# RWKV-7 and SwiGLU in one kernel: transposes as pairs of 64-row tiles, narrower Gram products, SwiGLU over two slices, a new order

## The chip, the cores and the metric

One core of a Trainium2 chip runs the whole program. The metric is the device time of one execution in microseconds (us), the median of several runs. In the profile PE is TensorE (its matmuls), PEld its weight loads, DVE is VectorE, ACT ScalarE, POOL GpSimd and SP SyncE, which here only issues DMAs.

## The reference

The first half is a recurrence over 768 tokens for 4 batches of 8 heads with head size 40. For each head there is a 40x40 state:

```python
for t in range(S):
    y[:, :, t] = np.einsum('bhd,bhde->bhe', rt, state)
    Sa = np.einsum('bhde,bhe->bhd', state, at)
    state_decay = state * wt[:, :, None, :] - np.einsum('bhd,bhe->bhde', Sa, bt)
    state = state_decay + np.einsum('bhd,bhe->bhde', vt, kt)
```

The second half takes `y` as 3072 tokens of 320 features, scales them by their root mean square and a gain, and computes `silu(x @ w_gate) * (x @ w_val) @ w_out` with an inner width of 1536. All arrays of the recurrence are float32; the three weight matrices and the gain come in as 64-bit floats and are narrowed to float32 in the kernel.

## The kernel before

**Chunks.** The 768 tokens are cut into 24 chunks of 32 (`C = 32`, `NCH = 24`), and all 32 sequences (4 x 8) are worked on at once. Inside a chunk the recurrence becomes products of small matrices. A step of a chunk is one call of `pe(...)`, `tt(...)`, `copy(...)` and so on; a `pe` step is a list of matmuls that is issued as a whole.

`front(c)` loads w, a, k, b and v of chunk c with the tokens on partitions, turns them round on TensorE (`turned`), and builds the products of keys within the chunk ("Gram" products, `gramk`) in levels of 1, 2, 4, 8 and 16 tokens; DVE scales keys and masks between levels. `inverse(c)` solves a 32x32 triangular system for each sequence on DVE, in 62 steps that depend on one another; the first four chunks (`EARLY`) do a half-sized version and finish on TensorE. `main(c)` carries the state over, forms `y`, and turns `y` twice (`turn4`, `turn3`) so that the features of 128 tokens lie on partitions in `xg`. `feed(g)` takes two chunks (256 columns) through the SwiGLU: 12 slices of 128 inner features in six pairs. For each slice there are two 64-row products (`h64`), four full ones (`h`), a Silu on ACT, a product on DVE and two products into the output (`out`). The weights of a slice come from DRAM (`sW`), 480 KB each, for every group again. `narrow` turns 64-bit weights into these slices at the start, in 24 parts.

**The transposes.** A transpose (`flip`) is a matmul whose stationary operand is the tile to be turned and whose moving operand is an identity. The profile shows it as one instruction at line 489, while every other float32 matmul (line 486) shows as two. `turned` makes eight flips for a tile of 128 partitions and 8 times 104 or 128 columns:

```python
def turned(t, at=lambda n: n, ins=P, outs=TOP):
    ps = plan.room().rearrange("p u f -> p (u f)").rearrange("p (n t) -> p n t", n=N)
    pe("turn", [flip(ps[0:outs, at(n), 0:ins], t[0:ins, n, 0:outs], ident[0:ins, 0:ins]) for n in range(N)])
    return ps
```

In each chunk there are such steps for w and a (`wan`), for k and b (`kbn`), for the scaled keys (`K`, 104 rows), for v and the solved part (`VU`) and for the state (`ST`, 104 rows), and one for r (`rn`) in every second chunk; `turn4` has four flips and `turn3` three.

**What the array is told.** Matmuls come in several tilings of the 128x128 array, which the profile shows as rows*columns of the stationary operand: 128*128 (`h`, `out`, all flips and the fillers), 64*128 (`h64`), 64-row by 64-column tiles (Gram, score, update, y0), 32x32 tiles (`lower`), 128-row by 64-column tiles (`level`) and 64 by 32 (`state`).

**The order.** Nothing is scheduled by the compiler. Every step is first recorded (`Plan.add`); then `Plan.issue` issues all of them in the order of a written-out text `ORDER`, in which each word is the number of a step counted from the first that is not yet issued. Each engine executes its own steps in that order. A "-" in the text issues a filler (`plan.warm`): a matmul of the identity with itself, which is used where TensorE would stand idle. `PAIRS` assigns three pairs of PSUM banks to the steps that ask for a `room`. A fourth pair (`po`) gathers the output of the SwiGLU.

Of the kernel before, what the change touches and what calls it, by code (L numbers as in the profile page):

```python
# [8 lines left out]
I32 = mybir.dt.int32  # L9
# [8 lines left out]
P = 128  # L18
C = 32
LEVELS = (1, 2, 4, 8, 16)  # L20
CG = 2
WB = 5
LEAD = 2
# [10 lines left out]
85 83 84 76 58 78 86 74 73 59 60 75 5 89 61 88 77 4 43 6 201 7 87 334 90 44 8 214 213 53 62 9 - - - - - - - - 93 18 10  # L34
567 335 557 11 12 13 79 14 15 94 566 80 210 16 95 558 108 17 200 - - - 97 96 19 20 100 21 2 22 101 23 98 25 568 202 24
26 107 112 57 - - - - - 102 106 111 124 27 209 122 392 103 109 52 119 113 104 54 578 569 577 155 199 125 110 105 204
120 - - - - - - 114 203 118 117 121 559 211 598 589 562 46 131 129 132 45 560 212 597 563 588 561 123 115 136 586 384
133 134 - - - - - 126 130 116 47 564 3 145 216 394 383 135 336 128 137 48 144 143 141 91 587 219 142 51 570 127 1005
565 146 138 337 55 573 579 281 393 220 582 608 571 390 234 239 607 572 583 580 380 574 251 222 38 221 609 575 581 42 -
- - - - - - - 223 82 226 339 64 379 227 338 39 81 139 224 263 149 576 238 153 56 249 247 590 206 584 228 382 237 591  # L40
593 272 40 233 232 381 154 0 593 32 139 390 204 228 591 388 234 249 247 - - 324 235 35 31 27 244 229 146 147 259 281
245 258 149 34 325 594 36 33 270 155 243 62 605 584 598 230 - 239 40 214 599 601 242 628 64 49 91 627 602 30 626 1135
600 28 48 257 603 29 241 68 150 255 65 0 1347 194 0 194 84 173 0 - - - 182 540 200 0 184 1 186 542 540 0 506 0 457 469
849 199 455 242 111 97 110 112 96 51 61 439 460 458 122 50 243 0 0 255 242 0 709 104 470 242 120 246 259 708 57 247
458 456 0 257 718 256 470 242 0 716 265 487 486 0 268 0 0 265 101 473 0 262 277 0 273 0 236 0 260 0 269 0 242 461 - -
- - - - - 237 0 240 0 278 242 252 0 242 252 0 90 0 0 98 99 246 0 0 230 440 0 230 94 93 457 440 231 - - - - - - - - -
240 441 244 0 44 0 468 440 255 0 450 468 269 469 0 257 214 439 238 213 203 0 257 203 93 449 92 0 0 234 - - - - - - - -
245 437 0 250 262 0 464 246 247 436 260 245 446 258 259 469 244 - - 255 471 465 468 470 466 0 269 215 255 478 466 93
94 264 95 96 266 97 0 97 470 1 2 98 99 0 0 96 467 97 469 98 468 251 265 99 470 100 471 101 441 102 103 258 104 105 260
106 - - - - - - - - - - - 0 106 107 471 108 0 108 502 503 472 0 108 109 110 111 0 0 0 0 0 - - 13 0 16 562 572 146 571  # L50
561 147 14 142 143 374 15 13 355 - - - 25 386 358 0 358 386 388 16 25 387 389 390 70 79 17 391 28 191 147 355 356 80
148 149 359 0 68 28 2 29 149 0 149 34 150 29 151 187 24 25 31 152 33 153 188 391 393 32 154 35 390 392 358 0 0 152 40
187 153 27 154 155 156 33 157 158 159 160 161 34 162 36 163 164 37 165 41 391 38 42 392 39 394 561 166 395 393 552 0
42 559 549 548 395 209 0 549 560 42 165 210 43 44 211 427 428 395 - - - 565 166 45 167 557 168 0 565 566 168 739 0 522
693 534 526 124 - - 0 526 124 139 0 535 681 682 579 0 535 545 547 140 536 138 141 0 547 545 555 543 578 0 558 520 567
- - - - - - 518 378 0 696 378 380 381 695 518 120 685 526 - - - - - - 522 686 379 527 382 136 530 383 554 529 121 - -
141 540 523 565 539 537 142 538 524 - - - - 145 525 148 534 149 152 154 551 535 147 555 - - 157 146 550 536 150 155
# [3 lines left out]
478 595 568 - - 35 830 594 567 820 38 36 - 476 37 571 366 570 0 605 356 433 434 435 436 120 437 0 317 318 319 320 441  # L61
321 322 323 355 456 324 458 459 442 4 357 325 457 326 327 443 328 0 443 328 329 330 331 357 0 35 0 330 2 37 450 359 3
36 358 331 332 357 333 356 0 462 330 461 464 448 331 332 468 364 447 463 31 467 476 458 333 365 334 335 0 425 439 441
302 426 436 0 6 439 2 0 435 332 2 436 443 444 0 448 332 442 334 443 333 340 449 0 32 297 329 342 330 - 3 338 33 341
334 0 332 331 0 332 293 441 0 438 0 436 293 333 336 295 337 309 438 338 1 375 342 310 365 374 515 27 292 0 362 26 28
44 339 29 34 292 27 32 338 0 646 29 34 336 32 0 439 64 315 647 646 339 440 441 63 340 0 287 413 312 313 623 12 414 314
415 315 416 608 624 32 417 480 418 625 419 420 421 316 626 638 33 0 312 417 625 418 - - - - 476 313 601 602 600 610
812 419 420 421 822 258 422 423 0 313 810 423 625 637 2 0 819 2 0 254 473 420 421 645 310 422 0 - - - - - 310 422 3
313 33 0 28 626 307 419 639 627 420 637 308 0 637 20 635 420 647 21 421 23 422 613 648 819 38 22 809 423 39 659 24 611
3 612 36 818 424 651 808 621 425 25 660 426 - 616 249 427 0 427 3 25 58 57 428 28 47 0 428 429 28 430 3 431 0 26 25  # L70
614 484 31 27 617 627 0 458 216 400 590 600 401 0 12 582 32 401 583 25 0 397 579 21 - - - - - - - - - 588 29 28 30 591
22 453 428 398 605 23 0 591 23 429 602 24 609 0 24 397 588 602 1 604 398 429 430 2 399 427 0 584 - - - - - - - - - - -
- - - 4 397 0 25 397 4 0 393 394 21 23 27 28 395 598 24 424 607 0 21 38 35 395 37 396 24 2 424 47 397 398 399 400 25
# [4 lines left out]
663 729 634 977 562 563 717 713 986 978 665 564 565 566 975 567 568 714 569 985 570 571 967 722 572 723 - 0 400 403  # L78
726 402 572 401 573 0 726 738 736 573 739 574 664 575 737 576 577 3 723 578 751 579 760 580 747 581 582 633 583 584 0
584 585 3 634 586 636 587 635 734 588 633 0 746 588 - - - - - 403 757 589 722 590 3 404 591 592 593 594 595 596 408  # L80
# [163 lines left out]
class Plan:  # L244
# [17 lines left out]
    def foot(self, ap):  # L262
# [9 lines left out]
        if key not in self.masks:  # L272
# [4 lines left out]
            self.masks[key] = m  # L277
        return p, p + dims[0][1], self.masks[key]

    def add(self, engine, kind, issue, outs, ins):  # L280
        me = len(self.pieces)
        k = self.count.get(self.stage, 0)
        self.count[self.stage] = k + 1
# [764 lines left out]
```

## Time and profile before

| | |
|---|---|
| three runs | 1061.87, 1062.71 and 1066.75 us, median 1062.71 |
| profiled execution, first to last instruction | 1060.6 us; its own time with what lies around the span is not listed, and the median of the three runs is 2.1 us over the span |
| PE busy | 1009.5 us (95%), 23406 matmuls |
| PEld busy | 829.3 us (78%) |
| DVE busy | 842.3 us (79%), 2861 instructions |
| ACT, POOL busy | 468.1 us (44%), 309.5 us (29%) |
| DMA | 143.35 MB, mean 135 GB/s |

Busy is the time in which at least one instruction of the engine, or of the group, is running. Matmuls overlap each other (one takes 200 to 450 ns from its start to its modelled end, but the next starts long before that), so what a step costs TensorE is read from the timeline: the start of the next step less its own start. The start column of the timeline is used for that below.

### The profile page before, as it was taken

The numbers are of one execution on the slowest core, as the hardware profiler recorded it, in microseconds if no ns is written. First come the engines' busy times: TensorE is split into PE (matmuls) and PEld (weight loads), VectorE is DVE, ScalarE is ACT, GpSimd is POOL, SyncE is SP. The second block draws the span as 40 slices with busy tenths as digits, with TensorE's granted clock in tenths as the row PEclk, the third lists the DMA queues.
The fourth block names the chain that finished last, engine by engine and source line by source line (L and its number), as shares of the span: only waits on it lengthen the run. The fifth ranks groups of instructions, "written<-read, shape, count | busy, mean of one in ns | idle before, by whom it ended". The sixth has DMA issues, their size and how long they took to land.

```text
span 1060.6 us, 53494 instructions
## 1 busy us (share of the span) xinstructions
PE 1009.5 (95%) x23406; PEld 829.3 (78%) x23406; DVE 842.3 (79%) x2861; ACT 468.1 (44%) x1043; POOL 309.5 (29%) x554
## 2 busy tenths in 40 slices
PE   7868999999999999999999999999999999999997
PEld 6767777777888778787778778787777888787875
DVE  8978878776868988898898798989889899787411
ACT  6856666643543534434443444434344443431211
POOL 8824413120532241241233241340331331110000
PEclk9777998999999999999999999999999999999999
DMA  9965458766565483655565555574555555443252
GB/s 168 216 155 133 77 127 207 211 123 178 127 140 126 106 173 96 150 134 125 123 155 129 135 132 114 122 160 119 137 126 126 138 137 138 100 132 102 80 162 68
DMA packets 172457, 143.35 MB, mean 135 GB/s; under 512 B 125504, under 2 KB 143872, under 8 KB 172224
## 3 DMA queue, kind: packets, MB, share of 16 engines
q1 hardware_dynamic: 153856, 116.96, 42.9%
q0 software_dynamic: 16192, 22.64, 12.1%
q8 instruction: 184, 3.01, 1.2%
q10 hardware_dynamic: 2176, 0.33, 0.3%
q14 instruction: 49, 0.40, 0.1%
HBM read 123.86 MB, written 15.99 MB: 132 GB/s over the span
## 4 chain that ended last, share of the span: by engine, by line
PE 72%; DVE 8%; DMA 4%; ACT 3%; issue 3%; POOL 2%; SPq 1%; DVEq 0%; ACTq 0%; POOLq 0%
PE ps L486 50%; PE po L486 13%; PE ps L489 8%; DMA wf<-sW 2%; DVE LT L444 1%; DVE y L444 1%; DVE tmp L444 1%; POOL kbn L483 1%; DVE Yi L444 1%; DVE K L444 1%; SPq L483 1%; DMA sY<-Yi 1%; ACT VU L467 1%; PE po L1015 0%; DVE Ab L444 0%
## 5 line engine op out<-in xcount | busy, mean ns | idle before, releaser
L486 PE MATMUL ps<-xg,wf 128*128 128x256 f32 (+1 forms) x1728 | 353.5, 390 | 4.0 <-DVE xg L444 2.0
L486 PEld LDWEIGHTS ps<-xg,wf 128*128 128x128 f32 (+1 forms) x1728 | 261.4, 188 | 57.2 <-issue 15.0
L486 PE MATMUL po<-wf,hT 128*128 128x320 f32 x576 | 183.1, 449 | 0.1
L464 ACT ACTIVATE sg<-ps 128x256 f32<-128x256 f32 x144 | 53.6, 382 | 228.2 <-PE ps L486 224.9
L444 DVE TENSOR_TENSOR tmp<-Yi,M 128x60 f32<-128x60 f32 (+24 forms) x620 | 130.7, 211 | 19.1 <-DMA M<-sB 5.9
L444 DVE TENSOR_TENSOR Yi<-Yi,tmp 128x60 f32<-128x60 f32 (+24 forms) x620 | 129.7, 209 | 12.7
L483 POOL DMA_DIRECT2D VU<-in_v_dram x92 | 53.2, 584 | 274.1 <-PE ps L486 141.8
L486 PEld LDWEIGHTS po<-wf,hT 128*128 128x128 f32 x576 | 102.5, 191 | 35.7 <-issue 4.1
L444 DVE TENSOR_TENSOR hT<-ps,sg 128x256 f32<-128x256 f32 x144 | 59.7, 420 | 67.2 <-ACT sg L464 66.4
L444 DVE TENSOR_TENSOR K<-K,T 128x512 f32<-128x512 f32 (+1 forms) x192 | 93.4, 496 | 8.3 <-PE ps L486 5.8
L486 PEld LDWEIGHTS ps<-Ab,K 40*64 40x64 f32 x4608 | 77.2, 138 | 28.1 <-issue 10.5
L467 ACT COPY K<-K 128x256 f32<-128x256 f32 (+1 forms) x168 | 71.7, 443 | 58.4 <-PE ps L486 39.2
L486 PE MATMUL ps<-Ab,K 40*64 40x56 f32 x4608 | 87.2, 224 | 9.7 <-issue 3.8
L444 DVE TENSOR_TENSOR As<-ps,msi 128x256 f32<-128x256 f32 (+1 forms) x186 | 78.9, 476 | 14.4 <-PE ps L486 13.8
L467 ACT COPY KN<-ps 128x640 f32<-128x640 f32 x96 | 66.1, 690 | 53.5 <-PE ps L489 23.3
L483 POOL DMA_DIRECT2D kbn<-in_b_dram x92 | 53.3, 583 | 96.7 <-PE ps L486 94.3
L486 PEld LDWEIGHTS ps<-As,KN 128*40 128x40 f32 x3072 | 66.5, 124 | 15.7 <-issue 10.4
L483 POOL DMA_DIRECT2D kbn<-in_k_dram x92 | 53.6, 585 | 82.7 <-PE ps L486 82.6
L486 PE MATMUL ps<-As,KN 128*40 128x32 f32 x3072 | 73.2, 205 | 3.1 <-issue 2.5
L483 POOL DMA_DIRECT2D wn<-in_w_dram x92 | 51.6, 567 | 62.7 <-DVE tmp L444 24.1
L444 DVE TENSOR_TENSOR y<-y,ps 128x256 f32<-128x256 f32 x119 | 50.0, 420 | 16.2 <-PE ps L486 13.7
L444 DVE COPY_PREDICATED LT<-near,ps 128x384 f32<-128x384 uint32 (+2 forms) x72 | 52.2, 725 | 2.6 <-PE ps L486 2.0
(133 smaller groups left out, 1546.0 us busy)
## 6 DMA issues: line engine op xcount, KB each, us to landing
wf<-sW SPq DMA_DIRECT2D x144, 480.0 KB, 3.9
M<-sB SPq DMA_DIRECT2D x80, 128.0 KB, 4.1
rn<-in_r_dram SPq DMA_DIRECT2D x24, 160.0 KB, 5.4
sW<-ex SPq DMA_DIRECT2D x16, 240.0 KB, 3.4
out_dram<-o SPq DMA_DIRECT2D x48, 80.0 KB, 4.2
kbn<-in_k_dram POOLq DMA_DIRECT2D x92, 40.0 KB, 3.9
kbn<-in_b_dram POOLq DMA_DIRECT2D x92, 40.0 KB, 4.1
wan<-in_a_dram POOLq DMA_DIRECT2D x46, 80.0 KB, 4.9
```

Of the source, the lines that this page charges most:

```text
L444: plan.add("DVE", kind, lambda at: fn(at(o), *m(at)), [o], aps(*args))
L464: plan.add("ACT", "act", lambda at: nc.scalar.activation(at(o), at(a), f, **kw), [o] + aps(acc), [a])
L467: plan.add("ACT", "copy", lambda at: nc.scalar.copy(at(o), at(a)), [o], [a])
L483: plan.add(by, "dma", lambda at: queue.dma_start(out=o, in_=i), [o], [i])
L486: return o, lhsT, rhs, lambda at: nc.tensor.matmul(at(o), lhsT, rhs, start=start, stop=stop, skip_group_check=True)
L489: return o, i, ident, lambda at: nc.tensor.transpose(at(o), i, ident)
```

## The change

- `turned` takes its tile as two halves of 64 partitions (or of 40 where the rest is padding) and makes 16 flips instead of 8. The two halves of a pair use the upper and the lower 64 rows of the array and write two different PSUM banks. A flip now moves 64 columns of the identity (40 for `K` and `ST`) where it moved 128 (104). `turn4` goes from 4 to 8 flips of 40 columns, `turn3` from 3 to 6 of 64. The layouts of `rE`, `r2` and `vut` follow, and the copy of `a` into `A` and `Ab` is made in four pieces instead of two.
- The Gram products of the levels 4, 8 and 16 load 60, 56 and 48 key columns instead of 64.
- In `feed`, both slices of a pair go through one Silu and one product of 512 columns instead of two of 256.
- The ring of weight slices has 6 tiles instead of 5, in group 0 only two of them serve the products, and the narrowing uses fixed tiles; `x` and `ex` have fewer buffers, `tmp` is half as wide.
- `ORDER` and `PAIRS` are new throughout. The text has 175 fillers where it had 151.

```diff
-WB = 5
-LEAD = 2
+WB = 6
...
-    def turned(t, at=lambda n: n, ins=P, outs=TOP):
-        ps = plan.room().rearrange("p u f -> p (u f)").rearrange("p (n t) -> p n t", n=N)
-        pe("turn", [flip(ps[0:outs, at(n), 0:ins], t[0:ins, n, 0:outs], ident[0:ins, 0:ins]) for n in range(N)])
+    def turned(t, at, outs=TOP, by=half, w=64):
+        ps = plan.room().rearrange("p u (n t) -> p u n t", n=N)
+        pe("turn", [flip(ps[0:outs, u, at(n), 0:w], t[by(u), n, 0:outs], ident[by(u), by(u)]) for n in range(N) for u in range(2)])
...
-            pe("gramk", [mm(gr[half(i), o, n, 0:16 + D], K[part(o), 2 * n + i].rearrange("p x s -> p (x s)"),
+            pe("gramk", [mm(gr[i * 64:i * 64 + 64 - l, o, n, 0:16 + D], K[part(o), 2 * n + i].rearrange("p x s -> p (x s)")[:, 0:64 - l],
                             A[part(o), 2 * n + i, 16:]) for n, i, o in each])
...
-             turned(K.rearrange("p (n i) x s -> p n (i x s)", i=2), ins=TOP, outs=P).rearrange("p n (o e) -> p n o e", o=2)[:, :, :, 0:D])
+             turned(K.rearrange("p (n i) x s -> p n (i x s)", i=2), lambda n: n, P, part, D).rearrange("p o n e -> p n o e")[:, :, :, 0:D])
...
-        pe("turn4", [flip(xn[:, m], y.rearrange("p (m c) t -> p m (c t)", m=4)[:, m], ident) for m in range(4)])
+        pe("turn4", [flip(xv[:, o, m], yt[part(o), m], ident[part(o), part(o)]) for m in range(4) for o in range(2)])
...
-        pe("turn3", [flip(ps[:, kt, :], x[:, kt * P:(kt + 1) * P], ident) for kt in range(KT)])
+        pe("turn3", [flip(ps[:, u, kt], x[half(u), kt * P:(kt + 1) * P], ident[half(u), half(u)]) for kt in range(KT) for u in range(2)])
...
             for e in range(2):
-                pe("h", [mm(h[e][:, q], wk[e][2 * q + kt], x[:, kt, :], False, kt == 1)
-                                           for q in range(2) for kt in range(2)])
-                act(sgs[:, e], h[e][:, 0], AF.Silu)
-                tt(hTs[:, e], h[e][:, 1], sgs[:, e], MUL)
-                pe("out", [mm(po[:, q, 0:DM], hTs[:, e, q * P:(q + 1) * P], wfs[e][:, 2 * P:2 * P + DM], f + e == 0, f + e == FT - 1)
-                                            for q in range(CG)])
+                pe("h", [mm(h[e][:, q], wk[e][2 * q + kt], x[:, kt, :], False, kt == 1) for q in range(2) for kt in range(2)])
+            act(sg, hh[:, 0], AF.Silu)
+            tt(hT, hh[:, 1], sg, MUL)
+            for e in range(2):
+                pe("out", [mm(po[:, q, 0:DM], hT[:, e * GT + q * P:e * GT + (q + 1) * P], wfs[e][:, 2 * P:2 * P + DM], f + e == 0, f + e == FT - 1)
+                           for q in range(CG)])
...
+    for f in range(FT):
+        narrow_slice(f)
     for c in range(-2, NCH):
```

More of the change, by code (lines that the diff above doesn't have):

```diff
@@ L278, in foot, with add @@
         return p, p + dims[0][1], self.masks[key]
-    def add(self, engine, kind, issue, outs, ins):
+    def add(self, engine, kind, issue, outs, ins, after=()):
         me = len(self.pieces)
@@ L489, in flip, with pe @@
         return o, i, ident, lambda at: nc.tensor.transpose(at(o), i, ident)
-    def pe(kind, steps, more=[]):
+    def pe(kind, steps, more=[], after=()):
         def issue(at):
@@ L494, in issue @@
                 s[3](at)
-        plan.add("PE", kind, issue, [s[0] for s in steps] + more, [x for s in steps for x in s[1:3]])
+        return plan.add("PE", kind, issue, [s[0] for s in steps] + more, [x for s in steps for x in s[1:3]], after)
     ident = const.tile([P, P], FP32, name="ident")
@@ L532 @@
     eye = const.tile([P, C // 4, C], FP32, name="eye")
-    row, column, bits, same = (vut_.tiles[0][:, k, 0:C].bitcast(I32) for k in range(4))
+    row, column, bits, same = (vut_.tiles[0][:, 0, k, 0:C].bitcast(I32) for k in range(4))
     same = same.bitcast(FP32)
@@ L594 @@
     Yi_ = Turns(2, [P, C // 4, C], "Yi")
[L595 to L596 removed]
+    tmp_ = Turns(2, [P, 80], "tmp")
+    rE_ = Turns(1, [P, 2, N, 2 * C], "rE")
     r2_ = Turns(1, [P, N, 2 * C], "r2")
@@ L623 @@
     seq = lambda i, q: slice((i * 2 + q) * N, (i * 2 + q + 1) * N)
+    top = lambda i, x: slice(i * 64 + x * C, i * 64 + x * C + HC)
     own = lambda i, n: rows(i, n // 4)
@@ L900, in main @@
             pe("y0", [mm(y0[part(o), i, n], Sd[part(i), (2 * n + o) * D:(2 * n + o + 1) * D],
-                                 R["rE"][part(o), n, i, tk] if i == o else R["r2"][part(i), n, tk]) for n, i, o in each])
+                                 R["rE"][part(o), i, n, tk] if i == o else R["r2"][part(i), n, tk]) for n, i, o in each])
         level(yl[:, 1], 3)
@@ L970, in feed, with wf_next, narrow @@
             dma(out[row:row + CG * C, :].rearrange("(q s) d -> s q d", q=CG), o[at:at + C])
-    def narrow(f, h, dst, srcs):
-        plan.stage = "narrow", 2 * f + h
-        n = dst.shape[1]
-        rw = wf_.next().bitcast(I32).rearrange("p (f w) -> p f w", w=2)[:, 0:n]
-        for to, src, load in srcs:
-            dma(to(rw).rearrange("p (k f) w -> p k f w", k=2) if load == "raw2" else to(rw),
-                src.bitcast(I32).rearrange("(k p) (f w) -> p k f w", k=2, w=2) if load == "raw2"
-                else src.bitcast(I32).rearrange("p (f w) -> p f w", w=2))
+    def wf_next(g, f):
+        return wf_.tiles[f % 2 if g == 0 else (g * FT + f) % WB]
+    words = lambda w: w.bitcast(I32).rearrange("p (f w) -> p f w", w=2)
+    def narrow(f, part, srcs):
+        k = 2 * f + part
+        plan.stage = "narrow", k
+        rw = wf_.tiles[k if k < 2 else 2 + (k - 2) % 4].bitcast(I32).rearrange("p (f w) -> p f w", w=2)
+        for to, src in srcs:
+            dma(to(rw), src)
         lo, hi, top = rw[:, :, 0], rw[:, :, 1], rw.bitcast(I16)[:, :, 3]
-        ex = ex_.next()[:, 0:n]
+        ex = ex_.next()[:, 0:WH]
         exf, low = ex.bitcast(FP32), lo.bitcast(FP32)
@@ L990, in narrow @@
         stt(exf, low, 2.0 ** 20, exf, ADD, MUL)
-        dma(dst, exf)
-    last, cut = slice(2 * P, DM), WF // 2 - 2 * P
+        dma(sW[f][:, part * WH:(part + 1) * WH], exf)
     def narrow_slice(f):
-        f0, f1 = f * P, (f + 1) * P
-        narrow(f, 0, sW[f][:, 0:2 * P + cut], [
-            (lambda t: t[:, 0:2 * P], moe_w_gate[0:2 * P, f0:f1], "raw2"),
-            (lambda t: t[:, 2 * P:], moe_w_out[f0:f1, 0:cut], "rawo")])
-        narrow(f, 1, sW[f][:, 2 * P + cut:], [
-            (lambda t: t[:, 0:DM - cut], moe_w_out[f0:f1, cut:], "rawp"),
-            (lambda t: t[:, DM - cut:DM - cut + 2 * P], moe_w_val[0:2 * P, f0:f1], "raw2"),
-            (lambda t: t[half(0), DM - cut + 2 * P:], moe_w_gate[last, f0:f1], "raw64"),
-            (lambda t: t[half(1), DM - cut + 2 * P:], moe_w_val[last, f0:f1], "raw64")])
+        gate, value, o = words(moe_w_gate)[:, f * P:(f + 1) * P], words(moe_w_val)[:, f * P:(f + 1) * P], words(moe_w_out[f * P:(f + 1) * P])
+        two = lambda t: t.rearrange("p (k f) w -> p k f w", k=2)
+        pair = lambda w: w[0:2 * P].rearrange("(k p) f w -> p k f w", k=2)
+        cut, last = WH - 2 * P, slice(2 * P, DM)
+        narrow(f, 0, [(lambda t: two(t[:, 0:2 * P]), pair(gate)), (lambda t: t[:, 2 * P:], o[:, 0:cut])])
+        narrow(f, 1, [(lambda t: t[:, 0:DM - cut], o[:, cut:]),
+                      (lambda t: two(t[:, DM - cut:DM - cut + 2 * P]), pair(value)),
+                      (lambda t: t[half(0), DM - cut + 2 * P:], gate[last]),
+                      (lambda t: t[half(1), DM - cut + 2 * P:], value[last])])
+    for f in range(FT):
+        narrow_slice(f)
     for c in range(-2, NCH):
```

182 lines of the change are left out of this document (96 added, 86 removed), and 320 rows, old and new, of the table ORDER.

## The prediction

> **What bounds the kernel now.** I read the page first: busy time, the slices, the chain that ended last.
>
> ```profile
> span 1060.6 us, 53494 instructions
> ...
> PE 1009.5 (95%) x23406; PEld 829.3 (78%) x23406; DVE 842.3 (79%) x2861; ACT 468.1 (44%) x1043; POOL 309.5 (29%) x554
> ...
> PE   7868999999999999999999999999999999999997
> ...
> PEclk9777998999999999999999999999999999999999
> ...
> PE 72%; DVE 8%; DMA 4%; ACT 3%; issue 3%; POOL 2%; SPq 1%; DVEq 0%; ACTq 0%; POOLq 0%
> ```
>
> TensorE is busy in nearly every slice after the first five, and 72% of the chain is its own work. Next the windows, cut where the stages change. The first product of the SwiGLU (`h64`) is at 130 us by the timeline.
>
> ```profile
> 130.27 1.14 PE L486 MATMUL ps<-xg,wf 64*128 64x256 f32 x8
> ```
>
> ```profile
> core 0: us, PE busy (x) PEld busy (x) DVE busy (x) ACT busy (x) POOL busy (x), PEclk, DMA share, GB/s
> 0.00:130.00 130.00, 105.32 (x2827) 94.63 (x2827) 109.43 (x325) 87.42 (x184) 75.99 (x155) 0.86 0.72 152
> 130.00:313.00 183.00, 177.08 (x4128) 143.53 (x4126) 138.02 (x474) 95.57 (x212) 50.15 (x86) 0.98 0.62 156
> 313.00:874.00 561.00, 548.28 (x13206) 448.14 (x13197) 487.45 (x1712) 235.03 (x532) 169.67 (x290) 1.00 0.57 132
> 874.00:1014.00 140.00, 137.72 (x3071) 112.18 (x3072) 102.45 (x339) 44.34 (x104) 13.71 (x24) 1.00 0.43 113
> 1014.00:1061.00 47.00, 41.13 (x192) 30.84 (x192) 4.91 (x12) 5.72 (x14) 0.00 (x0) 0.99 0.36 109
> ```
>
> Three stretches matter. Up to 130 us no engine is full and fillers pad TensorE: work taken off it there is worth nothing by itself. From 313 to 874 us, seven groups of two chunks, it is busy 97.7% of the time, DVE 86.9%. The last 47 us are SwiGLU alone. So the time from 130 us on follows TensorE's work, with DVE close behind: 80.1 us a group, of which DVE is busy 69.6 us.
>
> **What a step costs TensorE.** Busy time counts overlapping instructions once and mean durations count them several times, so I took start-to-start times from the timeline (first column).
>
> ```profile
> 602.29 1.99 PE L486 MATMUL ps<-xg,wf 128*128 128x256 f32 x8
> 604.21 0.79 PE L486 MATMUL ps<-Xs,LT 32*32 32x40 f32 x64
> 604.93 0.66 PE L489 MATMUL ps<-ident,y 128*128 128x128 f32 x4
> 605.43 1.24 PE L486 MATMUL po<-wf,hT 128*128 128x320 f32 x4
> 606.51 1.89 PE L486 MATMUL ps<-xg,wf 128*128 128x256 f32 x8
> 608.33 0.83 PE L486 MATMUL ps<-VU,KN 64*40 64x40 f32 x64
> 608.96 1.14 PE L486 MATMUL ps<-Ab,K 40*64 40x56 f32 x64
> 610.03 0.55 PE L489 MATMUL ps<-ident,x 128*128 128x128 f32 x3
> 610.44 1.08 PE L489 MATMUL ps<-ident,VU 128*104 128x128 f32 x8
> ```
>
> ```profile
> 430.96 1.89 PE L486 MATMUL ps<-xg,wf 128*128 128x256 f32 x8
> 432.69 1.24 PE L486 MATMUL po<-wf,hT 128*128 128x320 f32 x4
> ```
>
> ```profile
> 515.15 1.04 PE L489 MATMUL ps<-ident,kbn 128*104 128x128 f32 x8
> 516.12 0.79 PE L486 MATMUL ps<-Xs,LT 32*32 32x40 f32 x64
> ```
>
> ```profile
> 573.59 0.88 PE L489 MATMUL ps<-ident,ST 104*104 104x104 f32 x8
> 574.31 0.88 PE L489 MATMUL ps<-ident,K 104*128 104x104 f32 x8
> 575.12 1.15 PE L486 MATMUL ps<-Ab,K 40*64 40x56 f32 x64
> ```
>
> An `h` step takes 1.73 us between steps of its own tiling (430.96 to 432.69), 1.82 where another tiling follows (606.51 to 608.33), and 1.92 where another also precedes (602.29 to 604.21). So leaving a tiling costs 0.09 us, and entering one about 0.10 for a full float32 load, less for small loads (0.06 for `y`, below). The Trainium skill, page "TensorEngine Tiling (Array Packing)", section "Tiling Modes", says that changing the mode drains TensorE. The trace agrees at about 0.09 us a change; the page gives no size.
>
> Eight flips of `kbn` take 0.97 us and are followed by another tiling: 0.88 without that, 0.11 a flip of 128 columns, 0.85 ns a column. `ST` takes 0.72 and `K` 0.81 - 0.09 = 0.72 for eight flips of 104 columns: 0.09 a flip. `y` takes 0.50 for four after another tiling, 0.44 plus 0.06. So flips go by the columns that move, and the load is hidden: `K` loads 128 columns within 0.09 us. How long a flip's load is comes from its rows, beside those of two-instruction matmuls:
>
> ```profile
> L489 PEld LDWEIGHTS ps<-ident,y 128*128 128x128 f32 x96 | 10.8, 141 | 3.7 <-ACT K L467 1.1 <-DVE y L444 0.8 <-DVE hT L444 0.4
> L489 PEld LDWEIGHTS ps<-ident,rn 128*104 128x104 f32 x96 | 10.4, 130 | 1.3 <-ACT KN L467 0.4
> L486 PEld LDWEIGHTS ps<-xg,wf 128*128 128x128 f32 x1152 | 211.0, 190 | 39.4 <-issue 9.9 <-DVE hT L444 0.6
> L486 PEld LDWEIGHTS ps<-Ab,K 40*64 40x64 f32 x4608 | 77.2, 138 | 28.1 <-issue 10.5 <-ACT K L467 3.9 <-DVE tmp L444 2.8
> ```
>
> 24 more columns cost a flip's load 11 ns, 0.46 ns a column: 48 ns for 104 columns, 59 for 128. In the other matmuls 64 more columns cost 52 ns, 0.81 a column.
>
> **Do two halves run beside each other?** No flip does so yet. The nearest row is `h64`, the same 64*128 tiling:
>
> ```profile
> L486 PE MATMUL ps<-xg,wf 128*128 128x256 f32 x1152 | 275.5, 386 | 0.3 <-DVE hT L444 0.3
> ...
> L486 PE MATMUL ps<-xg,wf 64*128 64x256 f32 x576 | 80.4, 400 | 3.6 <-DVE xg L444 2.0 <-ACT VU L467 0.9 <-issue 0.5
> ```
>
> A full product of 256 columns takes 239 ns of busy time, a half one 140: two halves 279, not 478. They run together. So I price a pair of flips at the longer of its moving columns (64: 54 ns; 40: 34) and one load (48 or 59): 56 ns for `wan`, `kbn`, `VU`, `rn`, 59 for `K`, `y`, `x`, 49 for `ST`.
>
> **The sum, part by part, from 130 us on.** Counts of steps are those that stand behind the first `h64` in the two order texts, read against the steps in the order in which the code records them.
>
> Transposes. `wan`, `kbn`, `VU`, `rn`: 0.87 to 0.45, 70 steps, 29.4 us. `K`: 0.71 to 0.47, 20 steps, 4.8. `ST`: 0.71 to 0.39, 21 steps, 6.7. `y`: 0.44 to 0.24, 22 steps, 4.4. `x`: 0.33 to 0.18, 22 steps, 3.3. Together 49 us of the 129 us that line 489 is busy in this stretch:
>
> ```profile
> 130.00:1061.00 931.00, 129.46 (x1046) 109.87 (x1044) 1.00 0.55 133
> ```
>
> Bounds: with moving columns alone (pairs of 54 and 34) 30.8 + 8.8 + 9.2 + 6.7 + 3.6 = 59 us; with loads as long as the `K` row allows (89 ns for 128 columns, 72 for 104) 20.7 + 0 + 2.9 + 1.8 + 1.3 = 27. I take 49, since load and move are each read from a row.
>
> Gram. 64 products take 1.07 - 0.09 = 0.98 us, 61 ns for four that run together, near the load of 64 columns at 0.81 (52). With 60, 56 and 48 columns the load shrinks by 3, 6.5 and 13 ns, of which the last is stopped at some 10 by the 56 moving columns (48 ns): 16 fours x 19.5 ns = 0.31 us a chunk, 19 chunks left: 6 us. Between 0 and 7.
>
> Changes of tiling. All flips leave the tiling of `h` and `out`. The old order changes it 471 times from the first `h64` on, the new one 515 times: the new text puts flips next to `h64` or to one another. 44 changes at 0.09 to leave and some 0.05 to enter: 6 us lost. Were all 155 flip steps to stand alone, up to 310 changes would cost 43 us; the count excludes that.
>
> Fillers from there on are 40 before and 30 after: 2 us gained. Steps that moved across the mark: 1 us.
>
> SwiGLU of two slices. It takes no TensorE work. DVE's product:
>
> ```profile
> L444 DVE TENSOR_TENSOR hT<-ps,sg 128x256 f32<-128x256 f32 x144 | 59.7, 420 | 67.2 <-ACT sg L464 66.4
> ...
> L444 DVE TENSOR_TENSOR As<-ps,msi 128x512 f32<-128x512 f32 x42 | 28.4, 683 | 9.6 <-PE ps L486 9.6
> ```
>
> 144 x 0.420 = 60.5 becomes 72 x 0.683 (another 512-column product from PSUM) = 49.2: 11 us less, 0.9 a group. `out` now waits for a longer Silu and product, about 0.5 us more; the next `h` and the chunk's steps queued ahead of `out` cover it, and at the very end, without them, it costs that 0.5 once. The two extra copies of `a` (48 in all) go to ACT, 44% busy: nothing. One `x` buffer instead of two: the next use is a chunk, 40 us, later: nothing. The weight ring and its loads on SP: TensorE hardly waits for `wf` (row below), so nothing to gain. The start: before the first `h64` stand nearly as many steps as now (DVE 318 after 326, ACT 196 after 180, TensorE without fillers 68 after 67), so I leave it at 130 us.
>
> TensorE's work from 130 us on is then less by 49 + 6 + 2 + 1 - 6 = 52 us. **What is late next is DVE.**
>
> ```profile
> DVE y L444 <- PE ps L486: 8.9, 14, 1.9
> DVE hT L444 <- ACT sg L464: 8.7, 12, 1.3
> ```
>
> ```profile
> PE ps L486 <- DMA wf<-sW: 0.2, 1, 0.2
> ```
>
> The first two rows are of the seven middle groups, the third of the whole span. In the groups most of DVE's longest waits end on TensorE directly or through Silu, so they shrink with it, but not below nothing: of 80.1 us a group 69.6 are busy, 68.7 after. A group that is 4.4 us shorter (52 us over eleven groups and the end) leaves 75.7, with DVE at 91%. Two engines so full wait for each other more; I add 0.6 us a group, 6 in all, bounds 0 and 15. 1060.6 - 52 + 6 = 1014.6; with the 2.1 us between span and median: **1017 us**.
>
> **Rivals.** (a) DVE takes over: its waits stay at 10.5 us a group and only its own 0.9 goes. Eleven groups give 10 us: 1053. For it: 87% busy, and DVE's chain of 62 steps a chunk has its order. Against: its waits end on TensorE. It decides if DVE is over 93% in the middle.
>
> (b) Loads bound the pairs, at the 0.81 ns a column of the other matmuls: 84 ns a pair for 104 columns, 104 for 128. Then the first four kinds gain 70 x 0.20, `ST` 21 x 0.04, `y` and `x` 1 together, and `K` loses 20 x 0.12: 13 us instead of 49. TensorE gains 16 in all and DVE stays slack: 1047. Against: `K` loads 128 columns every 90 ns today. The Trainium skill, page "TensorE: Matmul & The Clock Gate", section "LDWEIGHTS (loading the stationary operand)", has a load take its columns divided by 1.2 in ns, 87 and 107 here, nearly this case; the `K` row contradicts it at 128 columns.
>
> (c) Slower: the halves of a flip pair do not overlap. Then 16 flips cost two of today's halves each time: 0.90 for `wan` and its like (loss 70 x 0.03), 0.94 for `K` (20 x 0.23), 0.78 for `ST` (21 x 0.07), `y` and `x` 0.02 each: 9 us lost, plus 6 for changes, less 9 for Gram, fillers and moved steps, and the order, made for shorter flips, adds waits of some 5: 1074. It decides where a pair takes over 108 ns. Against: `h64`. The change would then not do what its name says.
>
> (d) The new order meets later transfers or longer SwiGLU chains than it allows for: a wait of PE for `hT` or `wf` of 0.5 us in each of 72 pairs gives back 36 us: 1053. Against: no such wait now.
>
> **How the numbers follow.** Forecast 0.68, (a) 0.14, (b) 0.05, (c) 0.08, (d) 0.05. 0.5% is 5.3 us, about what a measurement of this kernel can tell. The forecast's own range is 1003 (no new waits, and 8 of the 10 us up to the upper bound of the flips) to 1032 (waits at 15, flips 6 less). To hold 8 in 10 it reaches into (a) and (d): 1003 to 1045. Faster by over 0.5%: forecast, (a), (b) and (d) but for a few parts in which they end near 1060: 0.88. Slower: (c) and one part of (d): 0.09. The rest 0.03.
>
> **What would show it.** Eight pairs of `VU` from start to start in 0.45 to 0.55 us and line 489's busy time near half; Gram steps of 0.93, 0.87 and 0.83 us without a change; 72 `hT` products near 0.68; PE busy in the middle near 97%, DVE near 91%; the first `h64` at about 130 us. Wrong: a flip pair at 100 ns or more, DVE over 93% with PE below 95%, or an `h64` that starts past 140 us.

## The result and the profile after

The changed kernel is slower: 1121.5 us (median of 4 runs, 1111.4 to 1124.9) against 1062.3 us for the kernel before (median of 4 runs), a ratio of 1.052 [1.044, 1.060]. The prediction was 1017 us, faster. Ratios in this document are taken over all runs of a pair, with a 95% interval, and need not equal the ratio of the two medians. Of one kernel below, new_reordered, two of the four runs were in a slower state and are left out of its ratio. The profiled run of the changed kernel took 1118.2 us, with a span of 1116.4 us.

The page of the kernel after: busy time, TensorE's slices, the clock it was granted, and the chain that ended last.

```profile
span 1116.4 us, 55783 instructions
...
PE 1010.8 (91%) x24670; PEld 814.7 (73%) x24670; DVE 836.8 (75%) x2789; ACT 451.8 (40%) x1019; POOL 309.5 (28%) x554
...
PE   6887889889989999899899999999889998999998
...
PEclk9887889899989999999999999998999998999999
...
PE 63%; DVE 11%; issue 9%; DMA 9%; POOL 4%; SPq 2%; ACT 1%; DVEq 0%; POOLq 0%; ACTq 0%
```

TensorE is busy for as long as before (1010.8 us against 1009.5), although each flip moves about half the columns. Its slices have eights in the middle where there were only nines, the granted clock dips again and again, and "issue", time in which an engine waited for nothing that the profile shows, has gone from 3% of the chain to 9%. The windows of the kernel after, cut at the same stages (columns as in the prediction):

```profile
130.00:313.00 183.00, 165.86 (x4101) 134.37 (x4090) 132.54 (x441) 86.36 (x196) 45.00 (x77) 0.91 0.55 137
313.00:896.00 583.00, 538.08 (x13728) 427.98 (x13725) 473.74 (x1629) 226.13 (x525) 171.01 (x292) 0.96 0.53 127
896.00:1056.00 160.00, 148.47 (x3601) 118.93 (x3602) 116.56 (x398) 48.94 (x110) 25.92 (x45) 0.95 0.46 118
```

In the middle TensorE is busy 92% of the time and DVE 81% (538.08 and 473.74 of 583). So DVE did not become the bound: nothing in the middle is full. What TensorE waits for is in the view of its waits (total us, times, longest). First the kernel before, then the kernel after:

```profile
PE ps L486 <- issue: 16.9, 25, 1.8
...
PE po L1015 <- issue: 0.4, 1, 0.4
```

```profile
PE ps L517 <- issue: 47.6, 40, 3.8
PE ps L520 <- issue: 9.0, 7, 2.7
...
PE po L517 <- issue: 2.1, 1, 2.1
```

17.3 us in 26 waits became 58.7 us in 48. All waits of TensorE together grew from 44.6 to 99.5 us, so three quarters of the growth are these. One of them in the timeline of TensorE after (start, duration, step, and the idle time before it in brackets):

```profile
914.60 1.24 PE L517 MATMUL po<-wf,hT 128*128 128x320 f32 x4
915.77 0.69 PE L520 MATMUL ps<-ident,K 40*128 40x40 f32 x16
916.29 0.63 PE L520 MATMUL ps<-ident,kbn 64*104 64x64 f32 x16
916.86 0.78 PE L517 MATMUL ps<-ST,aP 40*32 40x40 f32 x64
917.57 0.79 PE L517 MATMUL ps<-VU,LT 32*32 32x40 f32 x64
918.29 0.40 PE L520 MATMUL ps<-ident,x 64*128 64x64 f32 x6
918.62 1.15 PE L517 MATMUL ps<-A,K 40*64 40x56 f32 x64
919.70 0.26 PE L520 MATMUL ps<-ident,rn 64*104 64x64 f32 x1
922.71 1.09 PE L520 MATMUL ps<-ident,rn 64*104 64x64 f32 x15 [2.75 <-issue]
923.50 2.12 PE L517 MATMUL ps<-xg,wf 64*128 64x256 f32 x8
```

The flip step of `rn` stops for 2.75 us after the first of its 16 flips. The view names no tile and no transfer that it waited for. Ahead of it stands a run of short steps: from the flips of `K` at 915.77 on, some 460 instructions in 3.9 us (a weight load and a matmul for every count of the "x" column), 2.2 us for each 256. After the stop, `h64` takes 2.12 us instead of 1.14: half clock.

**What it waits for is its instructions.** The DMA part of the page lists a queue for them, first before, then after (queue, packets, MB, share):

```profile
q8 instruction: 184, 3.01, 1.2%
```

```profile
q8 instruction: 194, 3.18, 1.2%
```

A packet is 16 KB. TensorE runs 47,125 instructions before and 49,655 after (loads, matmuls and semaphore waits); by 256 that is 184 and 194, the two counts of packets. So each packet brings 256 instructions. The Trainium skill, page "Trainium Architecture — The Big Picture", section "The software stack", has instructions of 64 bytes, which fits, and streams that are moved into the engines when a program is loaded; the trace shows the transfers spread over the whole run. I counted TensorE's instructions in the trace up to each issue wait. In the eleven traces of this study 351 of 362 such waits fall at a count of 193 or 194 past a multiple of 256 (46 of 48 after, 26 of 26 before). I call these places marks. In the trace after, the transfer of a block starts 1.17 us (median; 3.4 us at the 95th percentile; in 17 of 194 blocks it starts ahead of the mark) after the mark before has been passed, takes 1.10 us, and where TensorE stood waiting, it went on 1.43 us after the landing. Together that is 3.7 us for 256 instructions, and a block with less work than that is at risk of a wait. How great the risk is, a count shows. I took the time from just after one mark to the next without the wait at either, from 30 us on:

```
time of a block   blocks before   of them with a wait   blocks after   of them with a wait
under 2.5 us            4                 2                 24                19
2.5 to 3.7 us          35                16                 30                14
3.7 us and more       141                 6                136                13
```

The shortest blocks mostly end in a wait in the kernel after, those of 2.5 to 3.7 us in about half of the cases, longer ones seldom. The change made 20 more of the shortest.

**And long waits lower the clock.** Half clock comes in steps of 3.41 us. I summed TensorE's idle time over each such window of the eleven traces (without a few windows at the ends):

```
state in a window  idle time in it   windows   half clock in the next one
full clock         under 1.0 us         2886        8
full clock         1.0 to 1.2 us          75       14
full clock         1.2 to 1.4 us          70       30
full clock         1.4 us or more        126      113
half clock         under 0.2 us          224       65
half clock         0.2 us or more        110      103
```

So 1.4 us of idle time within one window is nearly always enough, and half clock is seldom left after a window with 0.2 us or more (7 of 110). The Trainium skill, page "TensorE: Matmul & The Clock Gate", section "HAM oscillation — how this bites in real kernels", gives as the rule that idle gaps must not pass about 3.4 us. Here less than half of that costs the clock, and the measurement decides.

### The profile page after: what moved, and what is told of

The parts are those of the page before. It is cut to its first block, busy times and chain, and to the rows that moved or that the text cites. A ratio compares the mean times of both kernels' runs of the same rounds, so it can differ in the third digit from the quotient of the medians.

```text
span 1116.4 us, 55783 instructions
## 1 busy us (share of the span) xinstructions
PE 1010.8 (91%) x24670; PEld 814.7 (73%) x24670; DVE 836.8 (75%) x2789; ACT 451.8 (40%) x1019; POOL 309.5 (28%) x554
## 4 chain that ended last, share of the span: by engine, by line
PE 63%; DVE 11%; issue 9%; DMA 9%; POOL 4%; SPq 2%; ACT 1%; DVEq 0%; POOLq 0%; ACTq 0%
PE ps L517 43%; PE po L517 13%; PE ps L520 6%; SPq L514 2%; DMA sB<-LT 2%; DVE Yi L475 2%; DVE tmp L475 2%; PE po L1046 2%; DVE K L475 2%; DVE LT L475 1%; POOL kbn L514 1%; DMA wf<-sW 1%; DMA M<-sB 1%; DMA LT<-sY 1%; DVE y L475 1%
## 5 line engine op out<-in xcount | busy, mean ns | idle before, releaser
L517 PE MATMUL ps<-xg,wf 128*128 128x256 f32 (+1 forms) x1728 | 369.2, 406 | 4.6 <-issue 2.8
L517 PEld LDWEIGHTS ps<-xg,wf 128*128 128x128 f32 (+1 forms) x1728 | 271.9, 198 | 62.1 <-issue 20.5
L517 PE MATMUL po<-wf,hT 128*128 128x320 f32 x576 | 187.1, 465 | 2.2 <-issue 2.1
L517 PEld LDWEIGHTS po<-wf,hT 128*128 128x128 f32 x576 | 109.7, 200 | 43.0 <-issue 9.0
L495 ACT ACTIVATE sg<-ps 128x512 f32<-128x512 f32 x72 | 43.0, 597 | 200.8 <-PE ps L517 200.4
L475 DVE TENSOR_TENSOR As<-ps,msi 128x256 f32<-128x256 f32 (+1 forms) x186 | 82.0, 475 | 16.1 <-PE ps L517 13.2
L517 PE MATMUL ps<-Ab,K 40*60 40x56 f32 (+2 forms) x4608 | 81.8, 220 | 12.4 <-issue 8.2
L475 DVE TENSOR_TENSOR hT<-ps,sg 128x512 f32<-128x512 f32 x72 | 49.6, 689 | 56.3 <-ACT sg L495 55.9
L517 PEld LDWEIGHTS ps<-Ab,K 40*60 40x60 f32 (+2 forms) x4608 | 71.7, 131 | 27.2 <-issue 15.3
L1046 PE MATMUL po<-ident 128*128 128x128 f32 x350 | 65.2, 332 | 3.3 <-DVE po L548 3.3
```

The lines of the kernel that those rows point to most:

```text
L475: plan.add("DVE", kind, lambda at: fn(at(o), *m(at)), [o], aps(*args))
L495: plan.add("ACT", "act", lambda at: nc.scalar.activation(at(o), at(a), f, **kw), [o] + aps(acc), [a])
L517: return o, lhsT, rhs, lambda at: nc.tensor.matmul(at(o), lhsT, rhs, start=start, stop=stop, skip_group_check=True)
L1046: plan.warm = lambda: nc.tensor.matmul(po_[:, 0, DM:DM + P], ident, ident, start=False, stop=False, skip_group_check=True)
```

## The experiments

Each time is the median of the run's own executions, and is compared with the kernel before as it ran beside it on the same chip; three chips were used, which is why the kernel before reads 1055.7, 1065.0 or 1066.0 us.

For each trace I split the span in three. Time lost to the clock is the span times (1 - mean granted clock). Waits are the sum of TensorE's waits. The rest is its work at full clock. Waits at half clock are taken off twice, which makes the work too low: by 2 to 4 us in most kernels, 7.5 in old_order_paired, 12 in new_reordered and 19 in pairs_reordered. In us:

```
kernel             flips   span     waits  of them issue  lost to clock  work
before             whole   1060.6    44.6      17.3           22.3       993.7
after              pairs   1116.4    99.5      58.7           64.8       952.1
old_shift          whole   1098.7    64.9      36.6           38.5       995.3
old_shift_whole    whole   1073.2    47.4      18.8           24.7      1001.1
new_shift          pairs   1119.8   104.3      63.5           59.3       956.2
old_order_paired   pairs   1106.5    80.5      45.0           73.0       953.0
new_order_whole    whole   1101.8    71.2      39.9           35.3       995.3
new_no_reload      pairs   1075.9    77.7      46.7           51.6       946.6
new_reordered      pairs   1151.8   121.4      13.4           82.9       947.5
pairs_reordered    pairs   1175.2   132.7      24.1           94.0       948.5
old_gram           whole   1061.5    46.0      19.6           28.7       986.9
```

The work falls into two groups, 987 to 1001 us with whole flips and 947 to 956 us with pairs, whatever the order; with the double count put back, 988 to 1002 and 951 to 967 us. The pairs did save work, in every kernel that has them. What decides the time is the other two columns.

**old_shift: the kernel before, moved by 64 instructions.**

```diff
 ORDER = """
+- - - - - - - - - - - - - - - - 
```

> The kernel before with 16 fillers ahead of its first step, 64 TensorE instructions more, while TensorE waits for its first data; nothing else is changed. Fetch theory (TensorE's long waits with no releaser come at every 256th of its own instructions, where the next 256 have not been fetched, and the old order happens to have slow steps at those places): the 256-instruction marks fall on other steps. Counting the old steps' costs between the new marks, waits with the releaser 'issue' go from 17 us to about 33, each of 1 us or more is followed by 3.4 us at half clock, and the time rises to 1080-1100 us. Order theory (the new order's waits come from the order's data and transfers, the marks play no part): within 4 us of the kernel before, issue waits 17 us.

Measured: 1098.5 us against 1055.7, 1.039 [1.036, 1.043]. Its waits:

```profile
PE ps L487 <- issue: 31.8, 30, 2.6
...
PE po L1016 <- issue: 2.5, 1, 2.5
...
PE ps L490 <- issue: 2.3, 2, 1.2
```

36.6 us instead of 17.3. The sixteen fillers take 6.2 us at the start, the first flips come 4.3 us later than before, and the run is 43 us longer. None of the 33 issue waits is at a step where the kernel before had one. The old order, then, lies well where it is: at the one other position tried it waits twice as long.

**old_shift_whole: moved by 256 instructions.** The control: if it is the marks, a whole block must bring them back.

```diff
     with tc.manual_schedule():
+        for _ in range(64):
+            nc.tensor.matmul(po_[0:32, 0, DM:DM + 32], ident[0:32, 0:32], ident[0:32, 0:32], start=False, stop=False, skip_group_check=True)
         plan.issue(ORDER, PAIRS)
```

> The kernel before, its order unchanged, with 64 products of 32x32 of the identity ahead of everything: 256 TensorE instructions, where the earlier run put 64. Fetch theory (TensorE waits where its instruction count passes a multiple of 256, and the old order happens to fit where these marks lie): a shift by a whole 256 puts every mark back where it was, so 1054 to 1068 us, 15 to 22 us of issue waits and 40 to 60 us at half clock, like the kernel before. Rival (anything put in front disturbs the old order, wherever the marks lie): at least what the 64 instructions cost, 1090 us or more with over 30 us of issue waits.

Measured: 1073.0 us against 1065.0, 1.006 [1.002, 1.009]. Waits and clock:

```profile
PE ps L486 <- issue: 18.8, 24, 3.3
```

```profile
PEclk9888999999999999999999999999999999999999
```

Four times as many instructions in front cost a fifth of what 64 did (8 us instead of 43), and the issue waits are back at 18.8 us. Of the 24 waits, 15 are at a step where the kernel before had one, and 11 of the 18.8 us are in these. The median is 5 us above the window that I gave; the products in front take 6.9 us, and the first flips come 7 us later. The position against the marks explains both runs. That anything in front disturbs the order, the rival, does not.

**new_shift: the changed kernel, moved by 64 instructions.** The same line of fillers ahead of the new `ORDER`.

> The changed kernel with 16 fillers ahead of everything, 64 TensorE instructions, the shift that cost the kernel before 3.9%. Fetch theory: the new order does not fit the marks where they lie, so moving them changes little: 1095 to 1135 us, 45 to 65 us of issue waits. Rival (anything put in front disturbs an order): another 3 to 4%, 1150 us or more.

Measured: 1125.1 us, 1.055 [1.048, 1.061] of the time before, and 63.5 us of issue waits: not to be told from the changed kernel itself (1.052). Its order lies as badly at this position as at its own.

**old_order_paired: the flips alone, with the layouts and copies that follow from them, in the old order.**

```diff
-        pe("turn", [flip(ps[0:outs, at(n), 0:ins], t[0:ins, n, 0:outs], ident[0:ins, 0:ins]) for n in range(N)])
+        pe("turn", [flip(ps[0:outs, u, at(n), 0:w], t[by(u), n, 0:outs], ident[by(u), by(u)]) for n in range(N) for u in range(2)])
...
```

> The kernel before, with its own order, feed and Gram products, and only the transposes made as pairs of 64-row halves. Order theory: the gain that was forecast for the flips shows, less more changes of tiling: 1012-1025 us. Fetch theory: the halves add 2400 instructions and shift every mark; counted between the marks the waits for instructions come to about 45 us from the first SwiGLU product on (12 in the kernel before), half clock grows with them, and what the flips save (45 us) is given back: 1055-1080 us. Pairs theory (the paired flips as such make TensorE lose its clock): half clock without waits ahead of it, 1070 us or more.

Measured: 1113.2 us against 1055.7, 1.052 [1.046, 1.059]; the same ratio as the whole change. The fetch theory had about 45 us of issue waits from the first `h64` on; they are 36 us there and 45.0 in the whole run, and the time is 33 us over the upper end of its window. The largest of these waits, and the clock:

```profile
PE ps L489 <- issue: 40.2, 39, 3.2
PE ps L492 <- issue: 4.8, 3, 2.6
```

```profile
PEclk8666798999989989999999999998999998999999
```

The pairs take 41 us off the work (36 with the double count put back), add 28 us of issue waits and 8 of others, and the clock takes 51 us more than before, a third of it ahead of the first `h64`. The theory that pairs as such lose the clock also allowed this time, but it asked for half clock without waits: all 20 stretches of half clock that begin before the end follow a window with at least 1.0 us of idle time. Each flip step has twice as many instructions (32 instead of 16, for the eight-flip kinds) and shifts every mark behind it, in less time.

**new_order_whole: the new order with whole flips.** The edit above the other way round, in the changed kernel; all other parts of the change stay in it.

> The changed kernel with its new order, SwiGLU and Gram products, and only the transposes made whole again (8 flips of 128 rows). Pairs theory: waits and half clock go, 1060-1085 us. Fetch theory: fewer instructions and slower steps, but the order's slow steps still do not stand at the marks: issue waits 35-50 us instead of 59, the flips' 52 us come back: 1130-1155 us. Order theory: waits as in the changed kernel, 1165 us.

Measured: 1104.9 us against 1055.7, 1.046 [1.042, 1.050], with 39.9 us of issue waits. So neither the pairs nor the new order with the rest of the change needs the other to lose: both move the marks away from where they lay in the old order. The time was 25 us under what I expected.

**new_no_reload: fewer transfers beside the fetches.** From the third group on, `feed` loads a corner of 64 bytes of each weight slice instead of all of it, so the weights in use are those of older loads.

```diff
-                dma(wf, sW[f + e])
+                dma(wf, sW[f + e]) if g < 2 else dma(wf[0:1, 0:16], sW[f + e][0:1, 0:16])
```

> The changed kernel, but from group 2 on the weights of a slice are not loaded again (64 bytes instead of 480 KB); the products use what lies in the tiles, so the result is not the reference's. It halves the DMA traffic and leaves TensorE's instructions and order as they are. If a fetch is late because it queues behind other transfers: the fetch starts sooner after the mark (1.2 us in the median now), issue waits fall from 59 us to 30-45, time 1075-1100 us. If the time of a fetch is its own: issue waits 52-62 us, time 1105-1120 us.

Measured: 1070.2 us against 1055.7, 1.010 [1.005, 1.015]; 46.7 us of issue waits instead of 58.7, though the core moves 79 GB/s instead of 129. A fetch starts 0.97 us after its mark (median) instead of 1.17. Neither window that I gave held: the waits lie between the two, the time 5 us under the lower. Waiting behind other transfers is a part of it; four fifths of the issue waits remain at a DMA share of 0.35 instead of 0.53. Other waits fell by 10 us and the clock's share by 13; which transfers made these, the run does not separate.

**new_reordered: the changed kernel in an order that spreads short steps.** Only `ORDER` differs; it has 186 fillers instead of 175.

> The changed kernel with the same steps on every engine, step for step, in another order: searched again, from the new order, with a model that takes the durations of the trace, lets no 256 TensorE instructions pass in under 3.3 us (up to 4.8 in its draws), counts 0.09 us and a load for each change of tiling, and half clock for 3.4 us after a gap of 1.1 us. Fetch theory: short steps stand between long ones, so 20 to 35 us of issue waits instead of 58.7, 25 to 55 us at half clock instead of 132, and 1015 to 1045 us: faster than the kernel before by 1.5 to 4%. Rival (the pairs of flips or the wider SwiGLU cost the time by themselves, by loads or chains): 1085 us or more, whatever the order.

Measured: 1140.5 and 1154.5 us against 1065.0, 1.075 [1.064, 1.086]. The first half of the expectation held better than hoped, the second failed. Its waits:

```profile
PE ps L508 <- DVE y L463: 14.3, 12, 6.2
PE ps L505 <- DVE y L463: 11.1, 14, 1.9
PE ps L505 <- DMA LT<-sY: 8.9, 5, 3.8
PE ps L505 <- issue: 8.4, 7, 3.8
...
PE po L505 <- issue: 2.1, 1, 2.1
PE ps L508 <- issue: 2.0, 3, 0.9
```

Issue waits fell from 58.7 to 13.4 us, under those of the kernel before. So they go with the order of the steps, and not with the steps. How much of the fall is due to the spread of short steps, and how much to the time that other waits gave the fetches, the run does not separate. The other waits, most of them for DVE and for landings, grew from 41 to 108 us, and with them the clock's share to 83 us. The rival, that pairs cost time by themselves, had the time right and the reason wrong: the work is 947.5 us (960 with the double count put back).

**pairs_reordered: the same search with a better model.** The kernel of old_order_paired, again with `ORDER` alone changed.

> The kernel before with its flips in pairs (as in old_order_paired), in an order searched again from the old one: TensorE's, DVE's and ACT's steps may move, every DMA queue keeps its sequence. The model now also has what the failed search lacked: accesses of different engines to one PSUM tile go one after the other, a DMA waits for the one eight places before it on its kind of queue, the landing times are drawn from the traces, and half clock begins after 1.2 us of waiting within one window of 3.4 us and lasts until a window without waits. Fetch theory: issue waits 20 to 32 us instead of 45, half clock 60 to 100 us instead of 149, work without waits again near 951 us; time 1045 to 1090 us, 0.99 to 1.03 of the time before. Rival (flips in pairs cost time in themselves): 1100 us or more, as in old_order_paired.

Measured: 1177.4 us, 1.101 [1.094, 1.108]. Issue waits of 24.1 us are as expected; the work of 948.5 us seems so too, but is 967 with the double count put back. The other waits are 108.6 us and the clock takes 94. The time is the rival's, which gave 1100 us or more. In this page the clock is at five or six tenths through much of the first 150 us:

```profile
PEclk9655677799899998999999999999999999989999
```

My model of the other engines is too rough to order them, and what it still lacks I did not find. So whether an order exists in which the pairs win is open. What the two runs show is that fewer issue waits are not enough where the other waits grow: the marks and the chains of the other engines have to fit at once. That fitting them would give the 1017 us of the sum is therefore argued, not shown.

**old_gram: the Gram products alone, in the old order.**

```diff
-            pe("gramk", [mm(gr[half(i), o, n, 0:16 + D], K[part(o), 2 * n + i].rearrange("p x s -> p (x s)"),
+            pe("gramk", [mm(gr[i * 64:i * 64 + 64 - l, o, n, 0:16 + D], K[part(o), 2 * n + i].rearrange("p x s -> p (x s)")[:, 0:64 - l],
```

> The kernel before, order unchanged, with only the Gram products of 60, 56 and 48 columns. No instruction is added or taken away, so every mark of 256 instructions stays at the same step. Fetch theory: the shorter products give 5 to 7 us of work and lose 0 to 4 of it again to blocks that are now a little short: 0.994 to 1.000 of the time before, 15 to 20 us of issue waits. Rival (the old order is so finely fitted that any change of a duration breaks it): 1.01 or more with over 25 us of issue waits.

Measured: 1061.4 us against 1066.0, 0.995 [0.991, 0.998]: half a per cent faster than the kernel before, a small gain but outside the interval. The one part that adds no instruction keeps its gain, and its work is 6.8 us less than before. The issue waits, 19.6 us in all, hardly change, and 23 of the 32 are at a step where the kernel before had one:

```profile
PE ps L486 <- issue: 18.2, 30, 1.7
...
PE po L1015 <- issue: 1.4, 2, 0.8
```

## Why the prediction was wrong

**The parts were priced right.** Start-to-start times of the kernel after, near the tenth percentile: 447 ns for 16 flips of `kbn` (I had 0.45 us), 470 for `K` (0.47), 408 for `ST` (0.39); Gram 921, 876 and 800 ns (0.93, 0.87, 0.83). These are the fastest steps; `wan` and `VU` reach 491 and 493 ns where I had 0.45 us, and `x` 235 where I had 0.18. Two halves do run beside each other. The usual step is slower. Medians of all steps from the first `h64` on that ran at full clock and without a wait, in ns:

```
step           wan   kbn    VU    rn     K    ST     y     x
before         874   900   967   918   770   759   480   384
after          492   542   585   493   520   434   323   328
saved          382   358   382   425   250   325   157    56
in the sum     420   420   420   420   240   320   200   150
```

Times the counts of the sum, the savings are 43 us. These times contain the changes of tiling, so they stand against 49 less 6 in the sum: the total is right, though `x` saved a third of its price. The median Gram steps fell from 1085 ns to 1031, 978 and 934, close to the 48, 104 and 160 ns that I had. From the first `h64` on the work fell by 45 us; the sum had 52. Gram alone gave 6.8 us in old_gram, where I had 6. DVE's product is the size I took from another row:

```profile
L475 DVE TENSOR_TENSOR hT<-ps,sg 128x512 f32<-128x512 f32 x72 | 49.6, 689 | 56.3 <-ACT sg L495 55.9
```

One of my signs was badly chosen: I wanted the busy time of the flips' line near half of 129 us, and it is 93 us:

```profile
130.00:1117.00 987.00, 93.25 (x2146) 77.42 (x2146) 0.95 0.51 126
```

Busy time counts the long end of every step, flips at half clock, and steps that a wait has split in two; the start-to-start times are the fair reading.

**The step that failed is "So the time from 130 us on follows TensorE's work".** It holds only while instructions come as fast as TensorE runs them and the clock stays up, and I gave both a price of nothing without saying so. The rows to see it by were before me: idle time that ended "<-issue" at the weight loads (9.9 and 10.5 us in two quoted groups), and 3% of the chain. Cut at the first `h64` of each kernel (130.27 and 143.46 us), the difference of 55.8 us is:

```
                                     before   after   change   in the sum
up to the first h64                   130.3   143.5    +13.2       0
from it on: work at full clock        906.7   861.4    -45.3     -52
            issue waits                11.2    53.4    +42.2       0
            other waits                 8.9    18.8     +9.9      +6 (0 to 15)
            lost to the clock           3.5    39.3    +35.8       0
```

The last term that I had named, engines waiting for each other more often, is within its bounds. The two that I had not named are worth 78 us. They belong together: 1.4 us or more of idle time in a window was followed by half clock in 113 of 126 windows, and 32 of the 48 issue waits are over 1 us long (6 of 26 before).

**The start** was late too: the first `h64` at 143 us instead of 130, which I had listed as a sign of being wrong. Equal numbers of steps ahead of it were no evidence for equal time. The windows up to it, before and after:

```profile
0.00:130.27 130.27, 105.59 (x2828) 94.76 (x2829) 109.43 (x325) 87.42 (x184) 76.26 (x155) 0.86 0.72 152
```

```profile
0.00:143.46 143.46, 115.87 (x3136) 102.65 (x3136) 109.83 (x318) 91.40 (x198) 68.27 (x143) 0.82 0.67 147
```

By the same split, 7 of the 13 us are lost to the clock, 3 are waits (none of them issue waits) and 3 are work. With whole flips the changed kernel has its first `h64` at 138.3 us, so some 8 us come with the rest of the change and some 5 with the pairs. These are single executions: new_no_reload, which is the changed kernel up to there, has it at 144.8. Whether the order or the new ring of weight slices makes the 8 us I did not test.

**The rivals.** (a) is out: DVE is at 81%. (b) and (c) are out by the start-to-start times. (d) had the form of the loss, new waits spread over the run, but named `hT` and `wf`, and priced them at 36 us; TensorE's waits for these are 4.9 us in the whole span after. The case on the slower side, to which I gave 0.09, had the wrong mechanism. What no rival had was a limit that is counted in instructions, though the change does little else to TensorE than to replace each flip by two shorter ones.

## What to carry to other kernels

Divide TensorE's instructions into blocks as the page's instruction queue suggests, and look for blocks with little work. As an estimate from the medians above, 256 instructions need some 3.7 us, 14 ns each, and a flip pair of 56 ns with its four instructions is at that limit; blocks between 2.5 and 3.7 us waited in about half of the cases. Where the order of the steps is fixed, any edit that adds instructions moves all later fetches; test that alone by putting 64 idle instructions, and then 256, in front of the unchanged kernel. And price waits together with the clock: one that brings the idle time within a window of 3.41 us to 1.4 us costs, in most cases, at least one window at half clock, 1.7 us more.

## What was not expected of the hardware

- TensorE's instructions come in blocks of 256 during the run, and the next block is asked for late: 1.2 us (median) after the mark before is passed, with 1.1 us to land and 1.4 us until use.
- Sixteen fillers at the very start made a 1056 us kernel 3.9% slower; 256 instructions there cost 0.6%.
- Half clock begins after 1.4 us of idle time in a window of 3.41 us in 113 of 126 cases, after 1.2 to 1.4 us in 30 of 70, and is kept by 0.2 us: of 110 windows at half clock with that much, 103 were followed by another.
